# Loads in halves, two more PSUM banks and a moved product in the prologue of a Nystrom attention and two-MLP kernel

## The chip, the cores and the metric

The kernel runs on one core of a Trainium2 chip. The metric is device time in microseconds, the median of three runs; profiles and times below are of that one core. PE is the matmul engine (PEld its weight loads), DVE the vector engine, ACT the scalar engine, POOL the general one, SP the engine that issues the DMAs.

## What is computed

Nystrom attention with 32 landmarks over 4 batches of 8 heads (576 tokens, 64 columns), then two MLPs (512 to 2048 to 512) over the 2304 tokens:

```python
q_lm = q.reshape(B, H, m, S // m, D).mean(axis=3)      # m = 32, S = 576
k_lm = k.reshape(B, H, m, S // m, D).mean(axis=3)
A, Bm, C = sm(q, k_lm), sm(q_lm, k_lm), sm(q_lm, k)    # softmax of scaled scores
Z = Bm.T / (norm1(Bm) * norminf(Bm) + 1e-06)
for _ in range(6):
    Z = 2 * Z - Z @ Bm @ Z
x = A @ Z @ C @ v
h = x @ w_in;   x = (h - tanh(h)) @ w_out              # first MLP
h = x @ w_in2;  out = (h * tanh(softplus(h))) @ w_out2 # second MLP
```

All weights of the MLPs come as 64-bit floats.

## The kernel before

The work is cut into slots. A slot of the first stage (128 of them, 32 for each batch) takes 128 hidden units of the first MLP for half a batch: six matmuls of 288 columns into a tile `h` (L500 to L502), the nonlinearity on ACT and DVE (L551 on ACT comes first, then `th`, `q` and DVE's `g`), and, three slots later, twelve matmuls into four `y` tiles (L603 to L607). A slot needs the tile `P` of its group of four slots: `P[j]` is the attention's `Z C v` of the batch times a quarter of `w_in`, made by 8 block matmuls (L211, from `p_gen`), copied from PSUM by ACT (L479, once for each group of heads g) and by DVE (L481, the low part). Each `P` takes four of the kernel's weight blocks. The second MLP follows in slots of 384 tokens.

Weights are turned from 64-bit into 32-bit floats in blocks of 512 KB, called conversions here: SP loads a block (L115) into one of three `raw` buffers, ACT runs L131 and L137, DVE runs L144, and a block of `w_out` is then split by ACT (L99) and DVE (L100). SP issues the next load into a buffer when L144 has read it. The first MLP has 32 blocks, and the first 16 of these are converted beside the prologue.

The prologue is `attn_pre(0)`, which leads to `Z0`: loads of k and q for two groups of heads (one load each, 576 KB); a mean over 18 tokens on DVE (L246); landmark scores in two halves of 304 columns each (L211), each half into two `ps_m` banks; ACT copies them out (L279) and DVE takes maxima (L280, L283), of which `nb` (L290) is made; ACT's exponentials (L293, L296); transposes on PE (L307, L324), copied into the k buffers by ACT (L311, L327); `C v` into `pv` (L358); `B B^T` into `py` (L218), used by L378; five steps of the iteration (L218 on PE, L387 on DVE), a sixth into `v6`, and `Z0` by ACT (L404). DVE has a chain from the transposed B (L320) to the norms `n4` (L366), which scale `pv` (L370) and `py`. `ps_m` has two banks, `ps_h` two, `ps_y` four; the `y` banks are empty in the prologue.

Beside it runs `pa`, the query branch `attn_a(0, ·, 0)`: scores of q against the landmarks into the two `h` banks (L211), transpose, maximum, exponential, sum, division, transpose (L429 to L449) and the split tile `AT` (L99, L100), needed by the first slot.

A loop steps these generators in turn (`pre`, `pa`, a generator `cv` of conversions), and `pre` has priority over the others. A list scheduler then sets each engine's order from priorities and from a model of when operands are ready; on the chip each engine runs its list in order. From slot 116 the order is that of the code.

Of the kernel before, what the change touches and what calls it, by code (L numbers as in the profile page):

```python
# [8 lines left out]
F32 = mybir.dt.float32  # L9
# [5 lines left out]
ALU = mybir.AluOpType  # L15
AX = mybir.AxisListType
# [11 lines left out]
def kernel(  # L28
# [11 lines left out]
    nc = tc.nc  # L40
    B, NPAIR, _, S = qT.shape
    NG = NPAIR // 2
# [3 lines left out]
    R = S // M  # L46
# [19 lines left out]
    ps_y = ctx.enter_context(tc.tile_pool(name="ps_y", bufs=4, space=PSUM))  # L66
    ps_h = ctx.enter_context(tc.tile_pool(name="ps_h", bufs=2, space=PSUM))
    ps_m = ctx.enter_context(tc.tile_pool(name="ps_m", bufs=2, space=PSUM))
# [17 lines left out]
    V = nc.vector  # L86
# [120 lines left out]
    def blocks(outs, lhs, rhs):  # L207
        for c in range(4):
            for e in range(2):
                ps = slice(64 * e, 64 * e + 64)  # L210
                mm(outs[e][32 * c:32 * c + 32], lhs[ps, c, :], rhs(ps, c % 2, c // 2), start=True, stop=True,  # L211
                   tile_position=(64 * e, 32 * c))

    def heads(o, lhs, rhs):

        for c in range(4):
            ps = slice(32 * c, 32 * c + 32)
            mm(o[ps], lhs[ps], rhs[ps], start=True, stop=True, tile_position=(32 * c, 32 * c))  # L218

    ATt = {}  # L220
    adone = set()
    ZT = {}

    inp = {}

    def attn_load(b, g):
        r = inp[b, g] = {}
        r["q"] = in_p.tile([128, 2, S], F32, tag="q", name="q")
        r["k"] = in_p.tile([128, 2, S + M], F32, tag="k", name="k")
        nc.sync.dma_start(out=r["k"][:, :, 0:S], in_=kT[b, 2 * g:2 * g + 2].rearrange("a p s -> p a s"))  # L230
        nc.sync.dma_start(out=r["q"], in_=qT[b, 2 * g:2 * g + 2].rearrange("a p s -> p a s"))

    def v_load(b, g):
        t = in_p.tile([128, 5, 256], F32, tag="v", name="v")
        inp[b, g]["v"] = t
        cols = slice(256 * g, 256 * g + 256)
        nc.sync.dma_start(out=t[:, 0:4, :], in_=v[b, 0:512, cols].rearrange("(j p) c -> p j c", p=128))
        nc.sync.dma_start(out=t[0:64, 4, :], in_=v[b, 512:S, cols])

    def attn_pre(b):  # L240
        qs = [inp[b, g]["q"] for g in range(NG)]
        ks = [inp[b, g]["k"] for g in range(NG)]
        red = sm_p.tile([128, NG, 2, 2, M], F32, tag="red", name="red", bufs=1)

        def mean(g, x, t):
            V.tensor_reduce(out=red[:, g, x], in_=t[:, :, 0:S].rearrange("p a (m r) -> p a m r", r=R),  # L246
                            axis=AX.X, op=ALU.add)

        def scaled(g, x):
            if x == 0:  # L250
# [20 lines left out]
        for hf in range(2):  # L271
            for g in range(NG):
                inp[b, g]["c"] = c[:, g]
            pp = [ps_m.tile([128, 512], F32, tag="m", name="m") for g in range(NG)]
            blocks([p[:, 0:NH] for p in pp], QB, lambda ps, g, a: ks[g][ps, a, NH * hf:NH * hf + NH])
            yield 1
            n = NH - M * hf
            for g, p in enumerate(pp):
                A.activation(out=c[:, g, NH * hf:NH * hf + NH], in_=p[:, 0:NH], func=ACTF.Copy)  # L279
                V.tensor_reduce(out=mx[:, g, hf:hf + 1], in_=p[:, 0:n], axis=AX.X, op=ALU.max)  # L280
                yield 0
                if hf:
                    V.tensor_reduce(out=mx[:, g, 3:4], in_=p[:, n:NH], axis=AX.X, op=ALU.max)  # L283
                    yield 0
            yield 1
# [31 lines left out]
        bb = sm_p.tile([128, 2, NG, M], F32, tag="bb", name="bb", bufs=1)  # L317
# [30 lines left out]
                        in1=mask.rearrange("p (o a) m -> p o a m", o=1).to_broadcast([128, NG, 4, M]), op=ALU.mult)  # L348
        yield 1

        pv = ps_m.tile([128, 512], F32, tag="m", name="m")
        for g in range(NG):
            for j in range(5):
                n = 128 if j < 4 else 64
# [14 lines left out]
        for g in range(NG):  # L369
            A.activation(out=yv[:, g, 32:96], in_=pv[:, 64 * g:64 * g + 64], func=ACTF.Copy,  # L370
                         scale=n4[:, 2, g:g + 1])
        yield 1
        py = ps_m.tile([128, 512], F32, tag="m", name="m")
        for g in range(NG):
            heads(py[:, 32 * g:32 * g + 32], bb[:, 1, g, :], bb[:, 1, g, :])
        yield 1
        nr = n4.rearrange("p t (g o) -> p t g o", o=1)[:, 3]
        V.tensor_tensor(out=yv[:, :, 0:32], in0=py[:, 0:64].rearrange("p (g n) -> p g n", g=NG),  # L378
# [354 lines left out]
    if True:  # L733
# [17 lines left out]
        pa = both(attn_a, 0, 0, True)  # L751
        n = nc_ = 0
        live = {"pre": pre, "pa": pa}
        while live or nc_ < PREP:
            st = []
            if "pre" in live:
                st.append("pre")
            if n >= 8 and "pa" in live:
                st.append("pa")
            if n == 1:  # L760
                for g in range(NG):
                    v_load(0, g)
            gens = []
            for k in st:
                if part(live[k]):
                    gens.append(live[k])
                else:
                    del live[k]
            if "pre" not in live and ready and nc_ >= 4 + NPRE - 1:
                pg = p_gen(0, ready.pop(0))  # L770
                part(pg)
                gens.append(pg)
            if (nc_ < 4 + NPRE or (nc_ < PREP and "pre" not in live)):
                part(cv)
                gens.append(cv)
                nc_ += 1
            parts(gens)
            n += 1
# [124 lines left out]
```

## Time and profile before

| | us |
|---|---|
| three runs | 864.64, 866.72, 867.72 |
| median | 866.72 |
| the profiled execution | 864.62 |
| its span | 862.8 |
| PE busy in the span | 817.7 (95%) |
| DVE, ACT busy | 501.6, 497.1 (58% each) |

The span leaves 1.8 us around it. The profile is of an execution near the fastest of the runs, 2.1 us below their median. Busy shares are means over stages; the rows further down are read by stage. The trace lists each of the small fp32 matmuls of the prologue twice.

### The profile page before, as it was taken

The numbers are of one execution on the slowest core, as the hardware profiler recorded it, in microseconds if no ns is written. First come the engines' busy times: TensorE is split into PE (matmuls) and PEld (weight loads), VectorE is DVE, ScalarE is ACT, GpSimd is POOL, SyncE is SP. The second block draws the span as 40 slices with busy tenths as digits, with TensorE's granted clock in tenths as the row PEclk, the third lists the DMA queues.
The fourth block names the chain that finished last, engine by engine and source line by source line (L and its number), as shares of the span: only waits on it lengthen the run. The fifth ranks groups of instructions, "written<-read, shape, count | busy, mean of one in ns | idle before, by whom it ended". The sixth has DMA issues, their size and how long they took to land.

```text
span 862.8 us, 14979 instructions
## 1 busy us (share of the span) xinstructions
PE 817.7 (95%) x5656; PEld 708.2 (82%) x5656; DVE 501.6 (58%) x1154; ACT 497.1 (58%) x1234; POOL 174.3 (20%) x202
## 2 busy tenths in 40 slices
PE   3778789999999999999999999999999999999998
PEld 1435579888997899889899989999889999899996
DVE  5787989898879986889992896521111111211111
ACT  4786787788877887789884775333222222222221
POOL 0000000776667855880000000000000000000000
PEclk9998999999999999999999999999999999999999
DMA  8789614151404300153004573021001000100100
GB/s 294 239 271 309 239 51 138 51 181 51 139 1 154 126 2 30 63 182 102 30 1 152 190 220 119 1 64 56 19 1 52 22 1 28 37 1 1 38 1 36
DMA packets 34921, 79.62 MB, mean 92 GB/s; under 512 B 5408, under 2 KB 14112, under 8 KB 34848
## 3 DMA queue, kind: packets, MB, share of 16 engines
q1 hardware_dynamic: 34848, 78.66, 27.7%
q8 instruction: 44, 0.72, 0.3%
q14 instruction: 29, 0.24, 0.1%
HBM read 65.01 MB, written 13.63 MB: 91 GB/s over the span
## 4 chain that ended last, share of the span: by engine, by line
PE 77%; ACT 9%; DVE 7%; POOL 3%; issue 2%; DMA 1%; SPq 0%; DVEq 0%; ACTq 0%; POOLq 0%
PE y L631 7%; PE y L627 7%; PE y L626 7%; PE y L603 6%; PE h L526 5%; PE h L525 5%; PE h L524 5%; PE y L607 5%; PE y L604 5%; PE m L211 4%; PE h L500 3%; PE h L501 3%; PE h L502 3%; PE m L526 2%; PE m L525 2%; PE m L524 2%
## 5 line engine op out<-in xcount | busy, mean ns | idle before, releaser
L574 DVE TENSOR_TENSOR gg<-g,gg 128x384 fp32r<-128x384 f32 x96 | 53.5, 558 | 275.6 <-ACT g L573 275.6
L603 PE MATMUL y<-gg,w 128*128 128x288 f32 x512 | 151.6, 311 | 5.8 <-ACT gg L99 4.2
L604 PE MATMUL y<-gg,w 128*128 128x288 f32 x512 | 143.7, 296 | 0.0
L603 PEld LDWEIGHTS y<-gg,w 128*128 128x128 f32 x512 | 97.0, 189 | 30.7 <-issue 14.8
L607 PE MATMUL y<-gg,w 128*128 128x288 f32 x512 | 110.1, 300 | 1.9 <-DVE gg L100 1.5
L100 POOL TENSOR_TENSOR gg<-g,gg 128x288 fp32r<-128x288 f32 x80 | 69.0, 862 | 206.1 <-ACT gg L99 204.3
L572 ACT ACTIVATE gg<-h 128x384 fp32r<-128x384 f32 x66 | 32.5, 492 | 132.6 <-PE h L526 132.5
L627 PE MATMUL y<-w,gg 128*128 128x512 f32 x256 | 101.2, 395 | 0.0
L626 PE MATMUL y<-w,gg 128*128 128x512 f32 x256 | 100.8, 394 | 0.0
L604 PEld LDWEIGHTS y<-gg,w 128*128 128x128 f32 x512 | 97.3, 190 | 0.8 <-issue 0.8
L631 PE MATMUL y<-w,gg 128*128 128x512 f32 x256 | 88.4, 396 | 0.0
L607 PEld LDWEIGHTS y<-gg,w 128*128 128x128 f32 x512 | 81.7, 190 | 8.1 <-DVE gg L100 3.8
L500 PE MATMUL h<-AT,P 128*128 128x288 f32 x256 | 78.4, 306 | 6.2 <-DVE th L564 4.3
L557 POOL TENSOR_SCALAR mk<-s 128x288 uint8<-128x288 f32 x80 | 77.3, 966 | 7.2 <-ACT s L551 0.7
L502 PE MATMUL h<-AT,P 128*128 128x288 f32 x256 | 77.4, 303 | 0.2 <-DVE P L481 0.2
L501 PE MATMUL h<-AT,P 128*128 128x288 f32 x256 | 77.3, 302 | 0.0
L585 DVE COPY_PREDICATED g<-mk,th 128x288 f32<-128x288 uint8 x128 | 72.8, 569 | 4.6
L99 ACT ACTIVATE gg<-g 128x288 fp32r<-128x288 f32 x128 | 57.0, 445 | 25.0 <-PE y L607 17.3
L567 ACT ACTIVATE q<-q,bias_c 128x288 f32<-128x288 f32 x128 | 69.1, 540 | 2.2
L563 DVE TENSOR_TENSOR g<-h,s 128x288 f32<-128x288 f32 x128 | 57.3, 448 | 21.5 <-ACT th L552 20.9
L551 ACT ACTIVATE s<-h 128x288 f32<-128x288 f32 x128 | 52.4, 410 | 27.2 <-PE h L502 25.8
L572 ACT ACTIVATE gg<-m 128x384 fp32r<-128x384 f32 x30 | 14.8, 492 | 89.3 <-PE m L526 89.3
(154 smaller groups left out, 1858.2 us busy)
## 6 DMA issues: line engine op xcount, KB each, us to landing
w<-w1s SPq DMA_DIRECT2D x24, 512.0 KB, 4.4
raw<-in_w1i_dram SPq DMA_DIRECT2D x16, 512.0 KB, 5.6
raw<-in_w1o_dram SPq DMA_DIRECT2D x16, 512.0 KB, 4.5
raw<-in_w2i_dram SPq DMA_DIRECT2D x16, 512.0 KB, 4.4
raw<-in_w2o_dram SPq DMA_DIRECT2D x16, 512.0 KB, 4.1
k<-in_kT_dram SPq DMA_DIRECT2D x8, 576.0 KB, 6.0
q<-in_qT_dram SPq DMA_DIRECT2D x8, 576.0 KB, 5.8
ys<-raw SPq DMA_DIRECT2D x16, 288.0 KB, 2.3
```

Of the source, the lines that this page charges most:

```text
L500: mm(p, P[:, g, 0, c], AT[:, g, 0, :], start=(g == 0), stop=False)
L501: mm(p, P[:, g, 0, c], AT[:, g, 1, :], start=False, stop=False)
L502: mm(p, P[:, g, 1, c], AT[:, g, 0, :], start=False, stop=(g == NG - 1))
L557: eng.tensor_scalar(out=mk, in0=e, scalar1=FT, scalar2=None, op0=ALU.is_ge)
L567: A.activation(out=q, in_=q, func=ACTF.Square, scale=FB, bias=bias_c[:, 0:1])
L585: V.copy_predicated(out=g0, mask=mk0, data=t0)
L603: mm(yps[d], w[:, 0, c], gg[:, 0, :], start=(f == 0), stop=False)
L604: mm(yps[d], w[:, 1, c], gg[:, 0, :], start=False, stop=False)
L607: mm(yps[d], w[:, 0, c], gg[:, 1, :], start=False, stop=(f == NF - 1))
L626: mm(p, gg[:, 0, cs], w[:, 0, :], start=(f == 0), stop=False)
L627: mm(p, gg[:, 0, cs], w[:, 1, :], start=False, stop=False)
L631: mm(p, gg[:, 1, cs], w[:, 0, :], start=False, stop=(f == NF - 1))
```

## The change

For batch 0 the loads of k and q are issued as eight of 288 KB, one for each half of a group, and each half has a mean of its own. Also for batch 0 alone, the second half of the landmark scores goes to two `ps_y` banks. For every batch the matmuls of `py` stand ahead of those of `pv`. The query branch `pa` of batch 0 enters the loop at step 15, where it entered at step 8.

```diff
-        nc.sync.dma_start(out=r["k"][:, :, 0:S], in_=kT[b, 2 * g:2 * g + 2].rearrange("a p s -> p a s"))
-        nc.sync.dma_start(out=r["q"], in_=qT[b, 2 * g:2 * g + 2].rearrange("a p s -> p a s"))
+        for t, src in ((r["k"], kT), (r["q"], qT)):
+            if b:
+                nc.sync.dma_start(out=t[:, :, 0:S], in_=src[b, 2 * g:2 * g + 2].rearrange("a p s -> p a s"))
+            else:
+                for a in range(2):
+                    nc.sync.dma_start(out=t[:, a, 0:S], in_=src[b, 2 * g + a])
...
-            V.tensor_reduce(out=red[:, g, x], in_=t[:, :, 0:S].rearrange("p a (m r) -> p a m r", r=R),
-                            axis=AX.X, op=ALU.add)
+            if b:
+                V.tensor_reduce(out=red[:, g, x], in_=t[:, :, 0:S].rearrange("p a (m r) -> p a m r", r=R),
+                                axis=AX.X, op=ALU.add)
+            else:
+                for a in range(2):
+                    V.tensor_reduce(out=red[:, g, x, a], in_=t[:, a, 0:S].rearrange("p (m r) -> p m r", r=R),
+                                    axis=AX.X, op=ALU.add)
...
-            pp = [ps_m.tile([128, 512], F32, tag="m", name="m") for g in range(NG)]
+            if b == 0 and hf:
+                pp = [ps_y.tile([128, 512], F32, tag="y", name="y") for g in range(NG)]
+            else:
+                pp = [ps_m.tile([128, 512], F32, tag="m", name="m") for g in range(NG)]
...
+        py = ps_m.tile([128, 512], F32, tag="m", name="m")
+        for g in range(NG):
+            heads(py[:, 32 * g:32 * g + 32], bb[:, 1, g, :], bb[:, 1, g, :])
+        yield 1
         pv = ps_m.tile([128, 512], F32, tag="m", name="m")
...
-        yield 1
-        py = ps_m.tile([128, 512], F32, tag="m", name="m")
-        for g in range(NG):
-            heads(py[:, 32 * g:32 * g + 32], bb[:, 1, g, :], bb[:, 1, g, :])
...
-            if n >= 8 and "pa" in live:
+            if n >= 15 and "pa" in live:
```

What this makes of the engines' lists is seen at three places. On PE, from the start of the program (before, then after; `h` are scores of the query branch, `m` and `y` with `k,qb` the landmark scores, `m<-bb` is `py`, `m<-v,k` is `pv`):

```order
L211 MATMUL h<-q,kb 32x288
L211 MATMUL m<-k,qb 32x304 x2
L211 MATMUL h<-q,kb 32x288
L211 MATMUL m<-k,qb 32x304 x6
L211 MATMUL h<-q,kb 32x288 x6
L211 MATMUL m<-k,qb 32x304 x8
L307 MATMUL m<-ident,c 128x128 x8
L324 MATMUL m<-ident,c 64x128 x2
L358 MATMUL m<-v,k 32x64 x11
L218 MATMUL m<-bb 32x32
L358 MATMUL m<-v,k 32x64
L218 MATMUL m<-bb 32x32
```

```order
L211 MATMUL h<-q,kb 32x288
L211 MATMUL m<-k,qb 32x304 x2
L211 MATMUL y<-k,qb 32x304
L211 MATMUL m<-k,qb 32x304 x5
L211 MATMUL y<-k,qb 32x304 x2
L211 MATMUL m<-k,qb 32x304
L211 MATMUL y<-k,qb 32x304 x5
L211 MATMUL h<-q,kb 32x288 x7
L318 MATMUL m<-ident,c 128x128 x8
L335 MATMUL m<-ident,c 64x128 x2
L218 MATMUL m<-bb 32x32 x8
L373 MATMUL m<-v,k 32x64 x40
```

The second half of the landmark scores moved ahead of nearly all query scores, and `py`, which was interleaved one by one with `pv` eight times, now stands in one piece ahead of it.

On DVE, from the last means to `nb` and a little further (before, then after; `s` and `xm` are the query branch, `w<-y,raw` are conversions):

```order
L246 TENSOR_REDUCE red<-q 128x64
L429 STREAM_TRANSPOSE s<-h 128x288 x2
L280 TENSOR_REDUCE mx<-m 128x1 x2
L144 SCALAR_TENSOR_TENSOR w_155<-y,raw 128x512 x2
L432 TENSOR_REDUCE xm<-s 128x9
L280 TENSOR_REDUCE mx<-m 128x1
L283 TENSOR_REDUCE mx<-m 128x1
L280 TENSOR_REDUCE mx<-m 128x1
L283 TENSOR_REDUCE mx<-m 128x1
L287 TENSOR_TENSOR mx<-mx 128x2
L144 SCALAR_TENSOR_TENSOR w_173<-y,raw 128x512
L290 TENSOR_SCALAR nb<-mx 128x4
```

```order
L254 TENSOR_REDUCE red<-q 128x32 x2
L291 TENSOR_REDUCE mx<-m 128x1 x2
L291 TENSOR_REDUCE mx<-y 128x1
L294 TENSOR_REDUCE mx<-y 128x1
L291 TENSOR_REDUCE mx<-y 128x1
L294 TENSOR_REDUCE mx<-y 128x1
L298 TENSOR_TENSOR mx<-mx 128x2
L144 SCALAR_TENSOR_TENSOR w_161<-y,raw 128x512
L301 TENSOR_SCALAR nb<-mx 128x4
L144 SCALAR_TENSOR_TENSOR w_161<-y,raw 128x512
L440 STREAM_TRANSPOSE s<-h 128x288 x2
```

The query branch's transposes and maximum moved behind `nb`, and one conversion's L144 stands ahead of `nb` in place of three.

On ACT, from `Z0` to the second copy of the first `P` (before, then after):

```order
L404 ACTIVATE z<-m 128x128
L137 ACTIVATE raw<-raw 128x512
L99 ACTIVATE w<-y 128x512
L131 ACTIVATE y<-raw 128x512
L137 ACTIVATE raw<-raw 128x512
L99 ACTIVATE w<-y 128x512
L479 ACTIVATE P<-m 128x512
L99 ACTIVATE w<-y 128x512
L479 ACTIVATE P<-m 128x512
```

```order
L415 ACTIVATE z<-m 128x128
L131 ACTIVATE y<-raw 128x512
L137 ACTIVATE raw<-raw 128x512
L490 ACTIVATE P<-m 128x512
L131 ACTIVATE y<-raw 128x512
L137 ACTIVATE raw<-raw 128x512
L99 ACTIVATE w<-y 128x512
L131 ACTIVATE y<-raw 128x512
L137 ACTIVATE raw<-raw 128x512
L99 ACTIVATE w<-y 128x512
L490 ACTIVATE P<-m 128x512
```

Ten conversions have begun on ACT when it comes to `Z0` before, eight now; between the two copies of `P` stood one instruction, now six. Ahead of the first slot's L551 (L562 now) twelve conversions have begun in both programs. On SP the eight loads stand where four stood, ahead of the first weight blocks, which now each wait for an earlier load to have landed, since no ninth load is issued before the first has landed. On every engine the two lists differ up to about slot 13, and behind that only at single places.

## Rows read from the trace of the kernel before

**Rows 1.** Busy time by stretch: us, each engine's busy us, granted PE clock, DMA share, GB/s.

```profile
44.00:120.00 76.00, 60.62 (x321) 37.75 (x322) 62.20 (x142) 59.48 (x141) 0.00 (x0) 0.93 0.72 244
120.00:862.00 742.00, 732.53 (x5066) 658.67 (x5066) 411.07 (x941) 411.45 (x1034) 173.57 (x196) 1.00 0.21 67
```

**Rows 2.** Chain of waits that ended last, first 130 us: start, us, what.

```profile
17.35 0.55 ACT y L131
17.90 0.55 ACT raw L137
...
30.86 0.52 ACT yv L370 x2
...
40.23 0.28 ACT z L404
...
44.60 0.24 PE h L500
```

**Rows 3.** Instructions in order of time, loads and means: start, us, engine, line, operation, [idle before].

```profile
2.22 0.75 SPq L231 DMA_DIRECT2D q<-in_qT_dram  x1
...
4.85 1.35 DVE L246 TENSOR_REDUCE red<-k 128x64 f32<-128x1152 f32 x1 [3.31 <-DMA k<-in_kT_dram]
...
9.57 1.35 DVE L246 TENSOR_REDUCE red<-q 128x64 f32<-128x1152 f32 x1 [0.16 <-DMA q<-in_qT_dram]
...
16.25 0.45 DVE L432 TENSOR_REDUCE xm<-s 128x9 f32<-128x288 f32 x1
```

**Rows 4.** Instructions in order of time, from the landmark scores to the first exponential.

```profile
11.27 1.25 PE L211 MATMUL m<-k,qb 64*32 64x304 f32 x12 [1.03 <-ACT qb L253]
...
14.90 1.64 PE L211 MATMUL m<-k,qb 64*32 64x304 f32 x16 [1.42 <-DVE mx L280]
...
16.61 0.74 ACT L279 ACTIVATE c<-m 128x304 f32<-128x304 f32 x2 [1.66 <-PE m L211]
...
17.99 0.16 DVE L287 TENSOR_TENSOR mx<-mx 128x2 f32<-128x2 f32 x1
...
19.34 0.32 ACT L293 ACTIVATE c<-c,nb 128x32 f32<-128x32 f32 x1 [0.90 <-DVE nb L290]
```

**Rows 5.** Instructions in order of time, from the transposed B to `pv` and `py`.

```profile
22.88 0.23 DVE L320 STREAM_TRANSPOSE bb<-bb 128x64 f32<-128x64 f32 x1
...
23.81 0.86 PE L358 MATMUL m<-v,k 128*32 128x64 f32 x22 [0.40 <-ACT k L311]
...
26.59 0.16 DVE L366 TENSOR_TENSOR n<-n,rc 128x2 f32<-128x2 f32 x1
...
28.98 1.80 PE L358 MATMUL m<-v,k 64*32 64x64 f32 x44
...
31.22 0.86 PE L218 MATMUL m<-yv 32*32 32x96 f32 x16 [0.43 <-ACT yv L370]
```

**Rows 6.** Instructions in order of time, from `Z0` to the first slot's L551.

```profile
40.55 1.96 PE L211 MATMUL m<-w,z 64*32 64x512 f32 x16 [0.38 <-ACT z L404]
...
42.59 0.62 ACT L99 ACTIVATE w<-y 128x512 fp32r<-128x512 f32 x1
43.11 0.59 ACT L479 ACTIVATE P<-m 128x512 fp32r<-128x512 f32 x1
...
44.11 0.60 ACT L479 ACTIVATE P<-m 128x512 fp32r<-128x512 f32 x1
...
48.10 1.19 PE L211 MATMUL m<-q,kb 64*32 64x288 f32 x8
48.21 0.41 ACT L551 ACTIVATE s<-h 128x288 f32<-128x288 f32 x1 [2.37 <-PE h L502]
```

**Rows 7.** Busy time by stretch in the slots before 110 us, columns as in rows 1.

```profile
69.00:73.00 4.00, 4.00 (x14) 2.14 (x16) 3.49 (x11) 2.29 (x6) 0.00 (x0) 0.50 0.87 255
73.00:80.00 7.00, 5.82 (x39) 3.76 (x31) 1.68 (x5) 3.62 (x8) 0.00 (x0) 0.99 1.02 355
...
103.80:107.30 3.50, 3.46 (x20) 2.22 (x21) 3.50 (x10) 2.28 (x7) 0.00 (x0) 0.51 0.99 400
```

More of the change, by code (lines that the diff above doesn't have):

```diff
@@ L221 @@
     adone = set()
-    ZT = {}
     inp = {}
```

## The prediction, made before the changed kernel ran

> **What bounds the kernel now.** I read the busy time by stretch first. From 120 us on PE works 732.5 of 742 us at a granted clock of 1.00 [rows 1]: that part is PE at its peak, the two programs have nearly the same lists there, and whatever is won or lost ahead of it arrives at the end one for one. Ahead of it, from 44 to 120 us, no engine is full: PE 60.6, DVE 62.2, ACT 59.5 of 76 us [rows 1]. So I read the chain of waits for the first 130 us next. It hangs on the last load of q (until 9.57 [rows 3]), then goes through the scores, the exponentials, `pv`, the iteration, `Z0` at 40.23 and the two copies of `P` [rows 2, 6]. In that stretch the reader is to see one dependent chain that crosses engines, with other work (conversions, the query branch) slipped into each engine's list between its links. The timeline then shows where the links wait: for the second half of the scores PE sits idle 1.42 us until DVE's maxima free the banks [rows 4], and `pv` takes from 23.81 to 30.78 for work whose last 44 records take only 1.80 us [rows 5].
>
> **The change part by part,** against the profiled execution (864.62 us; the median of the runs lies 2.1 us higher).
>
> *Halves.* The last load of q lands as DVE begins at 9.57 after only 0.16 us of idle time [rows 3]: the loads set the pace, 576 KB every 1.57 us ((9.57 - 4.85) / 3). The same bytes in eight loads should land at the same end. A reduction of 1152 elements takes 1.35 us, one of 288 takes 0.45 [rows 3], so one of 576 lies near 0.75; only one such is left behind the last landing: 10.92 becomes 10.32, **0.6 us earlier**. Ends: 0.75 (nothing waits) and, if each of the four added loads delayed the last landing by an issue as long as that at 2.22 (0.75 [rows 3]), a loss of 3.0. I take 0.6, since eight issues of even 0.75 are over by 6.7, ahead of 9.57.
>
> *Banks.* With its own banks the second half no longer waits for DVE. PE has 26 records left when the last mean is in; 12 take 1.25 us and 16 take 1.64 [rows 4], 0.0975 for each further one, so 26 take 2.62. From 11.27 - 0.6 = 10.67 they end at 13.3, where before they ended at 16.54. ACT copies the second half out (0.74), and the maxima end 1.4 us after that copy begins (16.61 to 17.99 [rows 4]): 14.7. One L144 stands ahead of `nb` (0.69, as any L144; its ACT part is done by 14.6): `nb` is there by 15.6. But ACT's list now holds four conversion pieces between the copies and the exponentials, 0.55 each [rows 2]: 13.3 + 0.74 + 2.2 = 16.25. So ACT, not `nb`, is late, and the exponentials begin at 16.25 instead of 19.34 [rows 4]: **3.1 earlier**. If the third weight block landed late this would shrink; it was used at 17.35 with no wait for a DMA [rows 2], and its load is now issued at most 3 us later (four times 0.75), so I leave it.
>
> *Query branch later.* It took DVE and ACT time between the links. Behind the exponentials ACT now has one conversion piece and one of the branch's exponentials ahead of the first transposed copy, before it had two exponentials; DVE has one L144 and one reduction (0.45 [rows 3]) ahead of B's transpose. I charge 0.3: B's transpose at 20.1 instead of 22.88. From there to the last of `n4` took 3.87 us (22.88 to 26.75 [rows 5]); now one L144 less (0.7) and about 1.1 of the branch more: 24.35.
>
> *`py` ahead of `pv`.* The 80 records of `pv`, at 1.80 / 44 = 0.041 [rows 5], are 3.3 us; before they took 7.0, with `py` interleaved one by one. `py` alone is at most 0.86, the 16 records of the wider product [rows 5]. So 23.81 - 2.8 = 21.0, plus 0.9, plus 3.3: `pv` is complete at 25.2, after `n4` (24.35), so the order of these two is no new wait. ACT's scaled copy of it was at 30.86 [rows 2]: **5.7 earlier**. Bounds: 3.9 if half of the missing 3.7 us (7.0 - 3.3) has another cause than the interleaving and stays, 6.6 if `py` hides under the last copies.
>
> *The iteration* takes 9.37 us from that copy to `Z0` (30.86 to 40.23 [rows 2]); DVE's list has the same kinds and numbers of other pieces between its five steps, and I leave it. `Z0` at 34.5, 5.7 earlier.
>
> *What is late next.* `Z0` comes earlier than the conversions can follow. Eight of them have begun on ACT by then, ten before. So ACT does two more between `Z0` and the first slot, and now six of their pieces stand between the two copies of `P`. `Z0` to the block products' end is 0.32 + 1.96 us [rows 2, 6]: first copy at 36.7, then 0.5 for it, 4 × 0.55 and 2 × 0.52 (L99 to L479 [rows 6]): second copy at 40.5 instead of 44.11 [rows 6], **3.6 earlier**. Behind it wait DVE's low part (about 1.2 until it is done), a group of query scores on PE (1.19 [rows 6]) and five matmuls of 0.24 [rows 2] with their tail: about 3.9, against 4.1 from the second copy to L551 before [rows 6]. The first slot's L551 is at 44.4 instead of 48.21: **3.8 earlier**, with twelve conversions begun in both programs and so the same work ahead.
>
> *From there to 120 us* the same pieces remain in a somewhat other order. DVE and ACT have 14 and 16 us of slack there [rows 1], so an earlier start should carry through. I take the 3.8 unchanged. Ends: 0 (first rival) and 8 (second).
>
> The moved rows in later batches cost nothing: PE runs the same matmuls, and the bank that `py` takes earlier is wanted next by the iteration that needs `py` anyway. The `y` banks are empty until the first slots.
>
> **The sum.** 864.62 - 3.8 = 860.8 for a profiled execution, and 2.1 more for a median like that of the runs: **862.9**.
>
> **Rivals.** *Given back to the conversions.* Three buffers feed them. One turn of a buffer holds ACT for 1.1, DVE for 0.7 and, by the page's list of DMA issues, some 4.5 us for the landing; three share it, so 2.1 us each. If the second `P` has to wait for two conversions more than its start allows, 4.2 us are lost against 3.8 won. For it: at `Z0` the conversions are two behind. Against: from the first slot on the counts are equal. Midway, a gain of 1: **865.7**, within 0.3%.
>
> *More than the sum.* Early in the slots PE runs at half speed: 288 columns in 0.24 us at 44.60 [rows 2], which is 1.2 GHz, although the profile's clock of that time reads 1.00; and again from 69 to 73 and 103.8 to 107.3, at 0.50 and 0.51 [rows 7]. At 2.4 GHz each matmul costs 0.12 less. If an earlier, denser start spares both stretches (14 + 20 records), 4.1 more are won: **858.8**. For it: the first slots' nonlinearity is less broken up by conversions in the new list. Against: the idle gaps around them come from the conversions, which stay.
>
> *Slower: the low clock lasts longer.* The slots now run up against unfinished conversions, and PE may wait more often between its bursts. A slot of 18 matmuls costs 2.2 us more at 1.2 GHz than at 2.4. In the rows PE came back to 0.99 by 73 us [rows 7]. Three slots more at the low level undo the gain and make it slower by over 0.3%; four give 866.7 - 3.8 + 8.6 = **871.5**. Against: the lists hold the same conversions and slots, twelve conversions lie ahead of the first slot in both, and so no wait between slots need be longer than before. The Trainium skill (TensorE: Matmul & The Clock Gate, section on HAM oscillation) tells of a kernel whose PE falls back to the low clock again and again because it waits between bursts. By that, this rival decides the sign; the rows at 0.50 agree that it happens here.
>
> *The halves don't help.* If a load delays the landing by the longest issue whatever its size, q lands 3.0 later and everything behind it with it: a gain of 0.8 at most, **865.9**. Against: the fourth load's issue was over by 3.0, 6.6 us before the last landed [rows 3]. The Trainium skill (DMA: Bandwidth & Descriptors, section Bandwidth) speaks against splitting: it asks for transfers of at least 1 MiB and lists 0.95 us for 64 KB against 6.15 for 1 MB, so an estimate from that page is a fixed 0.6 for each load, 2.4 for four. By it the time would be near 865.3; no run here shows a lone load of that size.
>
> **How the numbers follow.** Forecast (a gain of 2.6 to 6) 0.54; more than the sum 0.16; given back 0.17; halves 0.05; low clock 0.08. A difference under 0.3%, 2.6 us, can't be told from none here. So faster by more than 0.3%: 0.70; within: 0.22; slower: 0.08. The range takes in the better rival with a microsecond beyond it and the given-back case up to a gain of 0.9: 857.8 to 865.8.
>
> **What would show it.** In the profile after: exponentials near 16.3, B's transpose near 20.1, `pv` in one piece of about 3.3 us and ACT's copy of it near 25.2, `Z0` near 34.5, six pieces between the copies of `P` and the second near 40.5, L551 of the first slot near 44.4, and every slot from 20 on some 3.8 us earlier. It would be wrong if the means still ended near 10.9 or later, if ACT waited for the third weight block, if `pv` stayed at several us, or if L551 came early but slot 20 did not.

## The result, and the profile after

| | before | after |
|---|---|---|
| runs of this comparison | 864.64, 866.72, 867.72, 868.38 | 859.15, 859.09, 855.77, 854.71 |
| median, us | 867.22 | 857.43 |
| profiled execution, us | 864.62 | 859.15 |
| its span, us | 862.8 | 857.4 |

The ratio is 0.9888, interval 0.9849 to 0.9928. The forecast was 862.9, its range 857.8 to 865.8: the direction was right, the time 0.4 us below the range. In two further comparisons the same kernel came out at 0.9934 and 0.992 (next section), so the true gain is nearer to 6 or 7 us than to 9.8. The profiled execution of before was the fastest of its four and that of after the slowest of its four; between those two the gain is 5.5 us.

Instructions of after in order of time (start, us, engine, line, operation, [idle before]), up to the exponentials; lines of after from L234 on stand 3 to 15 higher than those of before:

```profile
3.52 0.91 SPq L234 DMA_DIRECT2D q<-in_qT_dram  x2
...
9.12 1.50 DVE L254 TENSOR_REDUCE red<-q 128x32 f32<-128x576 f32 x2
...
10.65 0.26 ACT L261 ACTIVATE qb<-red 128x64 f32<-128x64 f32 x1 [1.11 <-DVE red L254]
...
10.96 0.74 PE L211 MATMUL m<-k,qb 64*32 64x304 f32 x5 [1.02 <-ACT qb L261]
...
12.31 0.42 ACT L290 ACTIVATE c<-m 128x304 f32<-128x304 f32 x1 [1.40 <-PE m L211]
12.63 0.66 ACT L131 ACTIVATE y<-raw 128x512 f32<-128x512 f32 x1
...
13.57 0.73 ACT L290 ACTIVATE c<-y 128x304 f32<-128x304 f32 x2
...
15.70 0.16 DVE L301 TENSOR_SCALAR nb<-mx 128x4 f32<-128x4 f32 x1
...
16.38 0.33 ACT L304 ACTIVATE c<-c,nb 128x32 f32<-128x32 f32 x1
```

The gap of 1.42 us on PE ahead of the second half of the scores [rows 4] is gone: the copies of the second half (`c<-y`) end at 14.30, and the exponentials begin at 16.38 where they began at 19.34. `nb` is there 0.52 us earlier than they begin: ACT, with its conversion pieces, is the late one.

The same view, from the transposed B to the scaled copy of `pv`:

```profile
20.30 0.23 DVE L331 STREAM_TRANSPOSE bb<-bb 128x64 f32<-128x64 f32 x1
...
20.84 0.43 PE L218 MATMUL m<-bb 32*32 32x32 f32 x16 [0.18 <-DVE BD L358]
...
21.21 2.83 PE L373 MATMUL m<-v,k 128*32 128x64 f32 x80
...
24.14 0.15 DVE L381 TENSOR_TENSOR n<-n,rc 128x2 f32<-128x2 f32 x1
...
24.39 0.52 ACT L385 ACTIVATE yv<-m,n 128x64 f32<-128x64 f32 x2
```

The 80 records of `pv` run in one piece of 2.83 us, where their interleaved run with `py` took 7.0 [rows 5], and the sixteen of `py` take 0.43 ahead of it. The copy stands at 24.39 instead of 30.86 [rows 2].

The same view, from `Z0` to the first slot:

```profile
33.73 0.28 ACT L415 ACTIVATE z<-m 128x128 f32<-128x128 f32 x1 [0.33 <-PE m L413]
...
36.11 0.60 ACT L490 ACTIVATE P<-m 128x512 fp32r<-128x512 f32 x1 [0.99 <-PE m L211]
...
39.51 0.48 DVE L440 STREAM_TRANSPOSE c<-m 128x288 f32<-128x288 f32 x1 [0.36 <-PE m L211]
39.89 0.58 ACT L490 ACTIVATE P<-m 128x512 fp32r<-128x512 f32 x1
...
40.05 1.18 PE L211 MATMUL m<-q,kb 64*32 64x288 f32 x8
...
41.09 0.68 DVE L492 TENSOR_TENSOR P<-m,P 128x512 fp32r<-128x512 f32 x1
41.16 0.61 PE L511 MATMUL h<-AT,P 128*128 128x288 f32 x1
...
42.29 0.68 PE L513 MATMUL h<-AT,P 128*128 128x288 f32 x2
...
42.77 0.41 ACT L562 ACTIVATE s<-h 128x288 f32<-128x288 f32 x1 [0.38 <-PE h L513]
```

The second copy of `P` is at 39.89 where it was at 44.11, the first slot at 42.77 where it was at 48.21 [rows 6]. After the second copy only 2.88 us pass, before 4.1: the group of query scores that starts at 40.05 waited for DVE's read of its bank (39.51), not for the low part of `P`, which DVE makes only at 41.09, while PE is at the end of that group and at the first of the five matmuls. The kernel before shows the same: its group began at 45.73, ahead of the end of the low part (45.82).

```profile
45.14 0.68 DVE L481 TENSOR_TENSOR P<-m,P 128x512 fp32r<-128x512 f32 x1
...
45.73 1.19 PE L211 MATMUL m<-q,kb 64*32 64x288 f32 x8
```

There the group stood behind seven matmuls of the slots (from 43.75, without a pause); after has done its first five and an earlier group of query scores while ACT was at the six pieces between the two copies (36.76 to 39.45).

The busy time by stretch (columns as in rows 1):

```profile
44.00:120.00 76.00, 63.39 (x328) 42.56 (x328) 63.45 (x150) 61.02 (x150) 0.00 (x0) 0.82 0.68 232
120.00:862.00 742.00, 727.47 (x5031) 654.18 (x5030) 407.36 (x924) 406.82 (x1021) 173.89 (x196) 1.00 0.20 66
```

In 44 to 120 us the granted clock is lower than before (0.82 against 0.93 [rows 1]), and yet more records of PE, DVE and ACT fall into the stretch. Behind 120 PE has 5.1 us less to do, which is the gain.

The chain of waits of after (start, us, what) has two links that the chain of before does not have:

```profile
25.42 5.36 DMA raw<-in_w1o_dram
30.80 0.66 ACT y L131
...
40.05 1.18 PE m L211 x8
...
47.29 0.59 DVE w L144
47.89 5.80 DMA raw<-in_w1i_dram
53.78 0.67 ACT y L131
54.45 0.55 ACT raw L137
55.02 0.70 DVE w L144
55.77 1.10 PE m L211 x4
```

A conversion's L144 (until 47.88) frees one of the three `raw` buffers, the load into it takes 5.80 us, and the next conversion, on which the next `P` hangs, starts when it lands. The list of waits, 20 to 76 us (engine, line, what for: us in total, times, longest), of before first:

```profile
ACT y L131 <- DMA raw<-in_w1i_dram: 0.9, 2, 0.6
ACT y L131 <- DMA raw<-in_w1o_dram: 0.3, 1, 0.3
```

and of after:

```profile
ACT y L131 <- DMA raw<-in_w1i_dram: 2.9, 2, 1.7
ACT y L131 <- DMA raw<-in_w1o_dram: 2.0, 1, 2.0
```

ACT's conversions wait for their blocks 4.9 us in after, 1.2 in before. (What this list leaves out is shown with the fourth buffer below.)

### The profile page after: what moved, and what is told of

It reads as the page before. It is cut to its first block, busy times and chain, and to the rows that moved or that the text cites. A ratio compares the mean times of both kernels' runs of the same rounds, so it can differ in the third digit from the quotient of the medians.

```text
span 857.4 us, 14989 instructions
## 1 busy us (share of the span) xinstructions
PE 816.9 (95%) x5656; PEld 709.6 (83%) x5656; DVE 503.3 (59%) x1158; ACT 497.3 (58%) x1234; POOL 174.6 (20%) x202
## 4 chain that ended last, share of the span: by engine, by line
PE 75%; ACT 9%; DVE 8%; POOL 3%; DMA 3%; issue 2%; SPq 0%; DVEq 0%; ACTq 0%; POOLq 0%
PE y L642 7%; PE y L638 7%; PE y L637 7%; PE y L614 6%; PE h L537 5%; PE h L536 5%; PE h L535 5%; PE y L618 5%; PE y L615 5%; PE m L211 3%; PE h L511 3%; PE m L537 2%; PE m L536 2%; PE m L535 2%; PE h L512 2%; PE h L513 2%
## 5 line engine op out<-in xcount | busy, mean ns | idle before, releaser
L511 PE MATMUL h<-AT,P 128*128 128x288 f32 x256 | 79.9, 312 | 6.5 <-DVE th L575 5.0
L512 PE MATMUL h<-AT,P 128*128 128x288 f32 x256 | 78.2, 305 | 0.0
L513 PE MATMUL h<-AT,P 128*128 128x288 f32 x256 | 77.8, 305 | 0.2 <-DVE P L492 0.2
L562 ACT ACTIVATE s<-h 128x288 f32<-128x288 f32 x128 | 52.7, 412 | 26.9 <-PE h L513 26.9
```

What stands on the lines that cost most here:

```text
L511: mm(p, P[:, g, 0, c], AT[:, g, 0, :], start=(g == 0), stop=False)
L512: mm(p, P[:, g, 0, c], AT[:, g, 1, :], start=False, stop=False)
L513: mm(p, P[:, g, 1, c], AT[:, g, 0, :], start=False, stop=(g == NG - 1))
```

## The experiments

The kernels ran in four groups, each on a chip together with runs of the kernel before; a ratio is against the runs of its group, and medians of different groups are compared with care.

**Repeats.** The kernel after in two more comparisons, each on a chip of its own, and a copy of the kernel before.

> The changed kernel once more, in five rounds. Two theories on the size of the gain. Shift alone: the chain of the prologue carries the gain, and the median lies 5 to 6 us (the shift of the slots from 13 on in the two profiles, 5.4) below the kernel before; the 9.8 us between the medians is then scatter of few runs. Shift and clock: executions differ by how long PE stays at the low clock in the slots before 120 us, the profiled execution of the changed kernel was one of its slow ones, and the median lies 8 to 10 us below.

> The kernel before, word for word, in five rounds against itself: both theories expect a ratio of 1 within 0.3%. Its profile tells whether stretches of PE at the low clock fall at the same places as in the first profile (shift alone expects the same places within 2 us; shift and clock expects other places, and a span that differs by 1 to 4 us with them).

> The changed kernel once more, on a third chip. If the true gain is the shift of the slots that the two profiled executions show (5.4 us) and the first median of 9.8 us was scatter, the ratio to the kernel before comes out at 0.993 to 0.995 and the single executions lie between 854 and 862 us. If the first median was right and the second an accident, 0.988 to 0.990.

| | runs, us | median | ratio, interval |
|---|---|---|---|
| a_again | 854.64 to 862.25 (8) | 860.35 | 0.9934, 0.9906 to 0.9961 |
| b_again | 862.52 to 868.25 (12) | 865.69 | 1.0012, 0.9996 to 1.0028 |
| a_third | 855.27 to 860.83 (6) | 857.75 | 0.992, 0.9897 to 0.9942 |

The 18 executions of after in three comparisons lie between 854.6 and 862.3, their median is 859.1; the kernel before had medians of 865.4 to 866.3 in the four groups. So the gain is near 6.7 us (865.8, the mean of these four medians, less 859.1; by 865.5, the median of all 81 executions of before in the groups, it is 6.4), and the first median of after was 1.7 below that of the 18 executions. a_again came out as the shift alone had it (5.0 us between the medians), a_third between the ranges of its two theories. The copy of before differs from before by 0.0012, so that a difference of this size can't be told from none. In its profile the low clock lies elsewhere (the lowest 12-us mean from 44 us on is 0.76 at 92 to 104, in before 0.78 at 68 to 80) and the span is 0.7 us longer: neither of the two theories had both.

**Each part alone, on the kernel before.** The edits, in this order: py, banks, halves, the branch begun later.

```diff
+        py = ps_m.tile([128, 512], F32, tag="m", name="m")     # ahead of pv
+        for g in range(NG):
+            heads(py[:, 32 * g:32 * g + 32], bb[:, 1, g, :], bb[:, 1, g, :])
+        yield 1
         pv = ps_m.tile([128, 512], F32, tag="m", name="m")
...
-            pp = [ps_m.tile([128, 512], F32, tag="m", name="m") for g in range(NG)]
+            if b == 0 and hf:
+                pp = [ps_y.tile([128, 512], F32, tag="y", name="y") for g in range(NG)]
...
+                for a in range(2):
+                    nc.sync.dma_start(out=t[:, a, 0:S], in_=src[b, 2 * g + a])
...
-            if n >= 8 and "pa" in live:
+            if n >= 15 and "pa" in live:
```

> The kernel before with py moved ahead of pv and nothing else. By the walk, pv is then complete some 2.8 us after the move's place (3.7 us of alternation less, 0.9 for py in front): Z0 near 37.4 in place of 40.23, and 1 to 3 us of the whole time. Rival: the norms on DVE end at 26.75 with two conversions in their list and then set the end, so that Z0 comes only 2.5 earlier or less and the conversions give all of it back: 0.

> The kernel before with two y banks for the second half of the scores and nothing else. By the walk the second half ends 2.5 us earlier (14.0 in place of 16.54) and the exponentials begin near 17, 2.3 earlier; pv is still interleaved, Z0 some 2 us earlier; 1 to 2 us of the whole time. Rival: the conversions and the query branch fill the time on ACT and DVE and Z0 moves by less than 1 us: 0.

> The kernel before with the loads and means of batch 0 in halves and nothing else. By the walk the last mean ends 0.6 us earlier; 0 to 0.6 us of the whole time. Rival from the page on DMAs: each load costs a fixed part, the last q lands up to 2.4 us later, and the time is 1 to 3 us longer.

> The kernel before with the query branch begun at step 15 and nothing else. By the walk this frees DVE ahead of nb by less than 1 us while the second half of the scores still waits for banks; 0 to 1 us of the whole time. Rival: the branch then ends late, AT is late for the first slot, and the time is 1 to 2 us longer.

**Parts left out of the kernel after.** py_banks has py and banks, without halves and without the later branch; no_py and no_banks are the kernel after with that one piece as it was in before. The edit shown is that of no_banks.

```diff
-            if b == 0 and hf:
-                pp = [ps_y.tile([128, 512], F32, tag="y", name="y") for g in range(NG)]
-            else:
-                pp = [ps_m.tile([128, 512], F32, tag="m", name="m") for g in range(NG)]
+            pp = [ps_m.tile([128, 512], F32, tag="m", name="m") for g in range(NG)]
```

> The kernel before with the two y banks and with py ahead of pv; the loads stay whole and the query branch begins at step 8. Alone the two brought 2.1 and 2.2 us and moved Z0 by 3.3 and 3.2 us. Theory: links of one chain add, and the halves and the later branch are worth next to nothing: Z0 at 33.8 to 34.5, the first slot's L551 at 42 to 43, ratio 0.993 to 0.9955 (a gain of 4 to 6 us), the same as the whole change within the intervals. Rival: the whole change gains more than its parts since the halves and the later branch are needed for the other two to count: ratio 0.996 to 0.998.

> The changed kernel with py behind pv again. Theory (the links add): the interleaving of pv with py is back, pv in some 7 us, ACT's copy of it near 27, Z0 near 37, the first slot near 45.5, ratio 0.995 to 0.997. Rival: without the order of py the rest brings what it brought alone, 1.6 to 2.6 us by the banks and nothing by the others: ratio 0.997 to 0.998; or py is worth more in company than alone and this kernel is at 1.0.

> The changed kernel with both halves of the scores in the same two banks. Theory (the links add): PE waits 1.4 us for DVE's maxima again, exponentials near 18 to 19, Z0 near 36.5, first slot near 45, ratio 0.995 to 0.997. Rival: with the query branch begun later DVE reads the maxima sooner, the wait is short, and the banks bring little: exponentials near 17 and ratio 0.993 to 0.994.

| | `Z0` in the profile | median, us | ratio, interval |
|---|---|---|---|
| before | 40.23 | 867.22 | 1 |
| only_pa | 40.37 | 865.39 | 0.9992, 0.9977 to 1.0007 |
| only_halves | 39.55 | 864.68 | 0.9994, 0.9978 to 1.0010 |
| only_banks | 36.96 | 862.75 | 0.9982, 0.9966 to 0.9997 |
| only_py | 37.06 | 863.23 | 0.9975, 0.9955 to 0.9995 |
| no_py | 37.22 | 860.35 | 0.9942, 0.9920 to 0.9964 |
| no_banks | 34.91 | 860.62 | 0.9944, 0.9927 to 0.9961 |
| py_banks | 36.04 | 860.88 | 0.9952, 0.9934 to 0.9970 |
| after | 33.73 | 857.43 | 0.9888, 0.9849 to 0.9928 |

The two large parts alone bring 1.6 and 2.2 us by their ratios (0.0018 and 0.0025 of 865.4), the two small ones 0.5 and 0.7, which can't be told from none; the banks alone (0.0018) stand little above the 0.0012 of the copy. Taken out of the whole, py and banks cost 1.7 and 1.8 us (6.7 less 0.0058 and 0.0056 of 866.3); py_banks has 4.2 of the gain (0.0048). Each interval is some 1.5 us wide to either side, so the links add as far as can be told: 1.6 + 2.2 + 0.5 + 0.7 = 5.0 us, and the small parts may be worth up to 2.5 in company. Whether the rest of 1.7 is real stays open. By the rival, that the two large parts need the small ones to count, py_banks would have been at 0.996 to 0.998; its value lies below that, but its interval reaches to 0.9970, the middle of it, so this rival is not excluded. no_py and no_banks gained a little more than the theory gave (0.995 to 0.997); no_banks has the exponentials at 18.28, as the theory had them, and not at 17. The expected `Z0` of py_banks, 33.8 to 34.5, was missed (36.04), and that of no_banks too (36.5, and 34.91 came): in one execution the links shift by more than a small part is worth.

Halves alone test the price of a load. The last mean and `qb` in the profile of only_halves:

```profile
9.65 1.51 DVE L255 TENSOR_REDUCE red<-q 128x32 f32<-128x576 f32 x2
...
11.20 0.26 ACT L262 ACTIVATE qb<-red 128x64 f32<-128x64 f32 x1 [1.13 <-DVE red L255]
```

Both halves of the last q are reduced back to back, 1.51 us, so that the last two landed nearly together; the whole one took 1.35 [rows 3]. In this execution `qb` was 0.24 us later than in before, in after 0.3 earlier. Over 18 profiles the start of `qb` has its median at 10.96 with whole loads (8 profiles, 10.42 to 11.13) and at 10.66 with halves (10 profiles, 10.36 to 11.36): the ranges overlap, so a gain of 0.3 is likely and not shown.

**The low clock.** warm adds matmuls whose results nobody reads, to keep PE busy in the waits of the iteration, behind the block products of the first `P` and between the first slots, for batch 0 alone.

```diff
...
+                for _ in range(3):
+                    mm(dum[0][0:96, 0:96], yv[:, 0], yv[:, 1], start=True, stop=True)
...
+            for _ in range(4):
+                mm(dum[0][:, 0:128], Z0.rearrange("p c m -> p (c m)"), ws[1][:, 1, 0:128], start=True, stop=True)
...
+        if s < 3:
+            for _ in range(4):
+                mm(dum[0][:, 0:HS], P[:, 1, 1, c], AT[:, 1, 0, :], start=True, stop=True)
```

> The changed kernel with matmuls added whose results nobody reads: three behind each step of the iteration, four behind the first P, four behind each of the first three slots, in a free y bank. They fill PE's idle time from 25 to 50 us. If the executions differ, and the gain varies, by how long PE stays at 1.2 GHz after the prologue, PE runs at 2.4 GHz from about 35 us on, and the median falls by 1 to 4 us against the changed kernel, with a smaller spread. Rival: PE's speed there does not matter since ACT, DVE and the loads set the pace; same time, or up to 1.5 us longer for the added matmuls.

It came to 857.85 us (855.67 to 861.92, 6 runs), ratio 0.9907, interval 0.9883 to 0.9930. That overlaps the intervals of both repeats of after; a gain of a microsecond can neither be shown nor excluded. Nor did the added matmuls hold the clock: the profile of warm has a mean of 0.89 from 44 to 120 us, and the three profiles of after have 0.82, 0.80 and 0.93. So this run does not tell what the low clock costs.

**A fourth buffer.** raw4 is the kernel after with the pair of edits below; bufs4 is the kernel after with the first alone; b_raw4 and b_bufs4 are the same edits on the kernel before; raw4_warm is raw4 with the matmuls of warm. By the second edit one more block is asked for ahead of its conversion.

```diff
-    raw_p = ctx.enter_context(tc.tile_pool(name="raw", bufs=3))
+    raw_p = ctx.enter_context(tc.tile_pool(name="raw", bufs=4))
...
-        ahead = 4 if more else 2
+        ahead = 4 if more else 3
```

> The changed kernel with four raw buffers in place of three and one more weight block fetched ahead. In the changed kernel ACT waits for weight blocks behind pv (1.95 us before the L131 at 30.80; 2.1 and 1.1 us in its second profile), so the conversions are the late link. If that sets the gain, the second copy of P comes at 38 or earlier and the time falls by a further 1 to 3 us against the changed kernel (about 857 to 859 where that one has 860.4). Rival: the waits lie beside other work, or the longer list of conversions ahead of P costs ACT what the DMA no longer does; within 1 us of the changed kernel.

> The changed kernel with the fourth buffer alone: the blocks are asked for in the prologue at the same steps as in the changed kernel. Theory: the buffers' turn round (a block waits for the conversion of the block three before it) is what held the loads back in the stage from 44 to 120 us, so the fourth buffer alone gives nearly all: 851 to 853 us. Rival: the early request is what counts, since the loads landed late at the first slots: 857 to 860 us.

> The kernel before with a fourth buffer for the weight blocks that wait to be converted, and its blocks asked for one step earlier in the prologue; nothing else of the change. Theory one: the loads of the weight blocks set the pace of the stage from 44 to 120 us in both kernels, and the prologue's gain comes on top, so this kernel gains what the fourth buffer gave the changed kernel (860.35 to 851.14, 9 us): 856 to 858 us, and the distance from it to the changed kernel with four buffers stays at 5 to 6 us. Rival: with four buffers the stage no longer follows the prologue's end, since its blocks are loaded by then, and the prologue's gain is lost: 851 to 853 us, as the changed kernel with four buffers. Second rival: the fourth buffer is worth something only where the prologue ends early: 863 to 866 us.

> The changed kernel with four buffers and, besides, the idle matmuls of the run warm in the prologue's chains and the first three slots. Theory: with four buffers no stretch after 44 us ran at the lower level of TensorE's clock, so idle matmuls have nothing to keep up there, and bring only what the prologue's own chains gain: 850 to 852 us, the same as with four buffers alone. Rival: the 2.5 us that idle matmuls brought the changed kernel come on top: 848 to 849 us.

> The kernel before with the fourth buffer alone, its blocks asked for at the same steps as before. The changed kernel gained 4.5 us by that buffer (857.75 to 853.24 on one chip). Theory one (the prologue's gain comes on top of the buffer's): this kernel is at 858.5 to 861, ratio 0.992 to 0.995, 5 to 7 us behind the changed kernel with the buffer. Rival (with enough buffers the stage up to 120 us no longer depends on when the prologue ends): 853 to 856, ratio 0.986 to 0.989.

| | median, us | ratio, interval |
|---|---|---|
| raw4 | 851.14 | 0.9834, 0.9808 to 0.9859 |
| raw4_warm | 852.04 | 0.9855, 0.9835 to 0.9875 |
| bufs4 | 853.24 | 0.9862, 0.9846 to 0.9878 |
| b_bufs4 | 854.88 | 0.9878, 0.9860 to 0.9895 |
| b_raw4 | 855.88 | 0.9892, 0.9875 to 0.9908 |

raw4 beats both kernels: 14.4 us by its ratio, at 851.1 where 857 to 859 was expected. The kernel before gains 9.3 us (b_raw4) and 10.6 (b_bufs4) by the buffer, more than by the whole change of the prologue. So the buffer's worth does not hang on the early prologue, against the second rival, and the gains do not simply add: b_bufs4, at 854.88, is where the rival had it and not where theory one did. With the fourth buffer the change is worth 1.4 us without the earlier request (0.9878 to 0.9862, the intervals overlap) and 5.0 with it (0.9892 to 0.9834). b_raw4 itself lies just under what theory one gave it. bufs4 and b_bufs4 ran on different chips, as did raw4 and b_raw4, so how much of the change is left beside the fourth buffer is not known better than by these two figures. Idle matmuls brought raw4 nothing.

The busy time by stretch, after and then raw4, shows what the buffer does:

```profile
44.00:56.00 12.00, 8.24 (x38) 5.07 (x40) 9.96 (x23) 10.27 (x24) 0.00 (x0) 0.69 0.88 293
56.00:68.00 12.00, 10.67 (x29) 5.39 (x26) 9.64 (x27) 10.01 (x24) 0.00 (x0) 0.59 0.80 250
```

```profile
44.00:56.00 12.00, 9.59 (x27) 3.53 (x28) 10.66 (x24) 10.95 (x24) 0.00 (x0) 1.00 0.95 300
56.00:68.00 12.00, 11.77 (x64) 7.29 (x64) 11.73 (x32) 12.00 (x30) 0.00 (x0) 1.00 1.03 393
```

From 56 to 68 us ACT is full, 12.00 of 12 us where it had 10.01, and the DMA moves 393 GB/s where it moved 250. The granted clock differs too, 1.00 where after had 0.59. The wait list of raw4 from 20 to 76 us has one line on these loads, 1.0 us where after had 4.9:

```profile
ACT y L131 <- DMA raw<-in_w1i_dram: 1.0, 1, 1.0
```

Neither the clock nor this wait explains what the buffer is worth in the kernel before. b_bufs4 won 10.6 us with 1.3 us of such waits, where before had 1.2, and at a lower clock, as the busy time from 44 to 98 us shows (before, then b_bufs4):

```profile
44.00:98.00 54.00, 44.13 (x208) 24.84 (x208) 42.53 (x96) 40.71 (x96) 0.00 (x0) 0.94 0.79 257
```

```profile
44.00:98.00 54.00, 48.64 (x238) 30.19 (x238) 49.31 (x112) 46.39 (x109) 0.00 (x0) 0.72 0.93 337
```

What the buffer changes is seen one step earlier, where SP waits for a conversion's L144 before it can issue the next load. From 44 to 112 us (before, then b_bufs4):

```profile
SPq L115 <- DVE w L144: 26.2, 11, 7.6
SPq L115 <- DVE y L144: 13.2, 5, 3.7
```

```profile
SPq L115 <- DVE w L144: 14.0, 6, 4.8
SPq L115 <- DVE y L144: 6.5, 4, 3.0
```

By 68 us, 19 to 21 conversions have begun on ACT in the 13 profiles with three buffers, whenever their prologue ended, and 23 to 25 in the five with four. The engines' lists change with the buffer as well (ahead of the first slot 16 conversions have begun in b_bufs4, 12 in before), and no run separates the list from the loads.

**What the end follows.** In the lists of ACT in order of time the last of the 32 conversions of the first MLP begins here, in before, after and raw4:

```profile
112.80 0.69 ACT L131 ACTIVATE y<-raw 128x512 f32<-128x512 f32 x1
```

```profile
107.95 0.70 ACT L131 ACTIVATE y<-raw 128x512 f32<-128x512 f32 x1
```

```profile
98.24 0.70 ACT L131 ACTIVATE y<-raw 128x512 f32<-128x512 f32 x1
```

The span ends 750.0, 749.5 and 749.0 us later. In 17 of the 18 profiles, this distance is 749.0 to 750.8 while the spans differ by 18.7; the exception is raw4_warm with 753.8, whose PE was 2 us less busy between 120 and 400 us. Slots and conversions stand in one list, so this instruction marks how far the list has come and need not be the cause. But by this row two profiles can be compared, and not by the first slot: that begins at 48.18 in bufs4, where after has 42.77, and at 50.13 in b_bufs4, where before has 48.21, and yet both end earlier. From the first slot to the last conversion it is 61.7 to 66.9 us in the 13 profiles with three buffers and 52.1 to 54.6 in the five with four.

## Why the prediction was wrong, step by step

Two terms of the sum were mis-sized: the stretch from the second copy of `P` to the first slot (3.9 us, with DVE's low part put ahead; it took 2.88), and the 2.1 us added to pass from a profiled execution to a median. And that the first slot's gain arrives at the end one for one was right in this pair of profiles and is not so in general.

**Halves.** Forecast 0.6 us earlier by the last mean; it ended at 10.62, forecast 10.32. By the medians over 18 profiles it is 0.3, within their scatter. The rival of a price for each load, 0.8 us left of the gain, fell: the loads did not land 3.0 later. The Trainium skill (DMA: Bandwidth & Descriptors, section Bandwidth) gave an estimate of 2.4 us lost for the four loads more (its table is of loads issued from GpSimd, where here SP issues them); only_halves, with 0.24 in the profile and a ratio of 0.9994, shows no such loss: in after the last issue is over at 4.43 (3.52 + 0.91, above), and the mean of its data begins with no wait at 9.87, so the loads are in flight together.

**Banks.** Exponentials at 16.38, forecast 16.25, with ACT and not `nb` as the late one, as forecast. B's transpose at 20.30, forecast 20.1.

**`py` ahead of `pv`.** One piece, as forecast, and shorter: 2.83 against 3.3, and `py` 0.43 against the bound of 0.86. The copy came at 24.39, forecast 25.2; `n4` at 24.29, forecast 24.35. The nearest row for the price, 0.041 us for a record at the tail of the interleaved stretch, was still dear; all 3.7 us of the interleaving went. The order is the cause: in no_py, interleaved again, a pair of the two products takes 0.59 us in the profile, and `pv` some 7 us.

**The iteration.** 9.34 us, forecast 9.37 as before. `Z0` at 33.73, forecast 34.5: the 0.8 of the step before.

**Late next.** First copy of `P` at 36.11 (36.7), six pieces between the copies as forecast, second copy at 39.89 (40.5). Then the step that failed: I had 3.9 us from there to the first slot, with DVE's low part (1.2) ahead of the group of query scores and the five matmuls. It took 2.88. The group started 0.16 us after the copy did, and the low part was made beside the matmuls; the rows of before, where the group starts ahead of the low part's end (above), did not bear out that term either. So the first slot moved by 5.4 us and not 3.8: 0.6 from ahead of the copy, 1.0 from this term.

**From there to 120 us** the gain went through one for one, as taken: 5.44 at the first slot, 4.85 at the last conversion, 5.4 in the span. There is luck in this: from the first slot to the last conversion a_again took 66.2 us and a_third 62.1, where this profile took 65.2 and before 64.6, so that first slots 5.4, 4.6 and 3.6 us earlier than in before became last conversions 4.9, 7.1 and 2.0 us earlier (after, a_third, a_again).

**The offset.** The sum was made for a profiled execution, 860.8, and 2.1 us were added since the profiled run of before lay that far under its median. The profiled run of after came to 859.15 and lay 1.7 above its median. The miss of 5.5 us is 1.65 from the sum (860.8 - 859.15) and 3.8 from this (2.1 + 1.7). Three runs of before, 3.1 us apart, said little on where a median lies, and nothing on the spread of after, whose 18 executions span 7.6 us. With the pooled median, 859.1, the forecast was 3.8 off and the time inside the range; the profiled execution of after lies on that median, so that the right offset was near 0, and the other 1.7 of the miss is that the first four executions of after lay low.

**The rivals.** *More than the sum* gave 858.8, near the time, but not by its mechanism: the low clock was not spared. After has 0.59 from 56 to 68 us (above), and its mean in 44 to 120 fell from 0.93 to 0.82. *Given back* is what began: the waits for weight blocks grew from 1.2 to 4.9 us. They did not eat the gain. One more buffer is worth 4.5 us to the kernel after (a_third to bufs4 on one chip). The rival's 4.5 us for a landing is the figure of the profile's list for the blocks of `w_out`; for those of `w_in` the list has 5.6. *The low clock lasts longer* happened in this execution, and yet the slots came earlier: in this pair a lower clock beside a chain that waits for loads did not cost the 2.2 us of a slot that I had charged. The Trainium skill (TensorE: Matmul & The Clock Gate, section on HAM oscillation) describes the fall back to the low clock between bursts; the rows agree that it happens, and no run here shows that it decided a sign.

**What stays open.** Why executions of after lie 7.6 us apart was not settled. They fall into two groups by the mean granted clock of the execution: at 0.974 to 0.979 or 0.994 to 0.996 the seven lie between 854.6 and 857.1, at 0.966 to 0.968 or 0.988 to 0.989 the eleven lie between 858.4 and 862.3. So a mean alone does not order them, but the pattern of the clock and the time go together. Two things differ between its profiles: the start of the exponentials (16.38, 17.09, 16.30 in the three profiles of after, following `qb` at 10.65, 11.36, 10.58) and the place of the low-clock stretches. Between the last and the first of these the exponentials differ by 0.08 us and the spans by 2.1 (855.3 and 857.4), so the start alone is not enough; the clock from 44 to 120 us is 0.82, 0.80 and 0.93 for spans of 857.4, 859.9 and 855.3. Whether the clock sets the time, or the waits set both, was not varied.

## What to carry to other kernels

When a chain gets shorter, look at once for what feeds it: after the change conversions waited 4.9 us for their blocks, before it 1.2, and one more buffer was worth more than the change. Don't read the worth of a buffer from the waits of the engine that uses it: the kernel before had only 1.2 us of them and won 10.6; the wait of the queue that has to issue the next load (39.4 us of 68, 20.5 with the fourth buffer) showed more. Take a forecast for a median from medians, and not from one profiled execution plus an offset of which nobody knows the cause. And find the row that moves with the end: here it was the last conversion and not the first slot, on which the forecast was built.

## What the runs showed of the hardware

Two products interleaved one by one on PE, one of 128 rows by 32 columns of the array and one of 32 by 32, took 7.0 us [rows 5] where one after the other they took 0.43 and 2.83, in after as in a_again and only_py. The stretches at the lower of the two clock levels move between executions of one kernel: the three profiles of after have their lowest 12-us mean from 44 us on at 56 to 68 (0.59), at 44 to 56 (0.62) and at 92 to 104 (0.72). And the granted clock of the first 46 us is not to be trusted in every profile: before has 1.00 there, up to 46, and yet matmuls of 288 columns follow each other in 0.24 us at 44.60 [rows 2], the lower level (1.2 GHz), where at 300 us, at a granted clock of 1.00, they follow in 0.13.
